# Converting 64-bit weights in seven VectorE instructions instead of nine, inside a Fourier and MoE kernel

## The chip, the cores and the metric

The kernel runs on one core of one Trainium2 chip. The metric is device time in microseconds for one execution, as the median of several runs. The runs of the kernel before took 2005.75, 2008.94 and 2009.99 us, so its median is 2008.94 us. The profiled execution is one more run, of 2006.93 us.

## The reference

Three layers follow one another on 4 x 3072 tokens of width 256. The code below leaves out the set-up of the inputs.

```python
# 1: Fourier layer
X = np.fft.rfft(x, axis=1)
Yr = X.real @ w_r - X.imag @ w_i + b_r
Yi = X.real @ w_i + X.imag @ w_r + b_i
Y = soft_threshold(Yr, 0.01) + 1j * soft_threshold(Yi, 0.01)
x = np.fft.irfft(Y, n=3072, axis=1)
# 2: MoE 1, w_in 256 x 2048, w_out 2048 x 256
h = x @ w_in
x = (h - np.tanh(h)) @ w_out
# 3: MoE 2, w_k 256 x 1024, w_v 1024 x 256, w_r 256 x 256
xk, xr = mix(x, x_prev, mu_k), mix(x, x_prev, mu_r)
k = np.maximum(xk @ w_k, 0.0)
out = sigmoid(xr @ w_r) * (k * k @ w_v)
```

The weights `w_in`, `w_out`, `w_k`, `w_v` and `w_r` of the two MoE layers arrive as 64-bit floats. The kernel reads each as a pair of 32-bit integers, a low and a high word side by side, and makes a 32-bit float of it.

## The kernel before, in words

**Stage 1** is the Fourier layer. The transform of length 3072 is split into factors 96 and 32. Each of the 4 batches has 12 *units* (`reg_unit`), so there are 48. A unit's work goes back and forth between the engines: `g` (TensorE, twiddles) to `xh`, `xl` (ScalarE and VectorE, the high and the low part of a value, lines 345 and 348), to `y` (TensorE, the weights `wh`, `wl`, two blocks of 12 matmuls), to `t` and `c` (VectorE, lines 529 to 534, bias and soft threshold), to `zh`, `zl` (ScalarE and VectorE), to `v` (TensorE, the inverse transform, two groups of three matmuls), to a copy and a store on ScalarE and SyncE's queue (`vdr`). A product of two 32-bit values is made from the high and low parts in three matmuls. When a batch is through, its `v` rows are loaded again as `vp`, multiplied by `e_sb` into `a` and stored as tokens (`ydr`, `reg_ap`). This work of batch b lies among the units of batch b+1, and that of the last batch among the first chunks of stage 2.

**Stage 2** (MoE 1) goes over 24 chunks of 512 tokens, with 8 pairs of weight slices in each. **Stage 3** is MoE 2. Both make products with fewer matmuls by using sums of blocks (`reg_forms`): for each slice of weights the kernel loads a 128 x 512 tile `ws` from DRAM (`stage`, line 690), adds and subtracts 128 x 256 blocks into `sq` (line 686), and splits these into high and low parts `ah`, `al`, `wh`, `wl`. The tokens get the same treatment: `yr` is loaded, `yt` holds the sums, and `yh`, `yl` the parts.

**The conversion** is `reg_conv(i)`, lines 597 to 632, once for each of 25 tiles of 128 x 512 weights. A DMA loads `raw`, 512 KB. Nine VectorE instructions make a 32-bit float of each pair. The result goes to DRAM as `wdr` (line 632, SyncE's queue), from where `stage` loads it as `ws`. The first 16 (`EARLY`: `w_in` and `w_out`) are converted during stage 1. Their load is issued on GpSimd's queue (line 613) into the one buffer of `raw` in the pool `px`; `cq` has two buffers there, `cs` and `cl` one each. The other 9 are converted in stage 2, with `raw` in the tile `sq` of the pool `pw` and the work tiles among the four buffers of `ws`. The pool `pw` takes the place of `px` (line 326), so the first load into `ws` can be issued only behind the last use of `px`, and that is the store of the last early conversion.

**Who sets the order.** Nothing is written down in the order in which it runs. Every instruction is registered with a priority and a cost in nanoseconds (`c_dve`, `c_act`, and for a DMA a fixed start of 650 ns, 290 bytes per ns on one common line and 950 ns to landing), and `_Plan.run` (lines 186 to 309) simulates the engines with these costs and emits each engine's instructions in the order of their simulated starts. On the chip each engine then runs its list in order. A different number of VectorE instructions, or a different last reader of a buffer, so gives other lists on all engines. Early conversions have priorities from 1000 on, which lets them into the gaps that the units leave in the simulation.

Of the kernel before, what the change touches and what calls it, by code (L numbers as in the profile page):

```python
# [8 lines left out]
F32 = mybir.dt.float32  # L9
F32R = mybir.dt.float32r  # L10
I32 = mybir.dt.int32
ACTF = mybir.ActivationFunctionType
ALU = mybir.AluOpType
# [135 lines left out]
class _Plan:  # L149
# [6 lines left out]
    def op(self, eng, dur, emit, prio, writes=(), reads=(), after=(), lat=SEM, seq=True, nbytes=0):  # L156
        o = _Op()
        o.nbytes = nbytes
        o.eng, o.dur, o.emit, o.prio, o.lat = eng, dur, emit, prio, lat
        o.idx = len(self.ops)  # L160
        o.start = o.end = None
        deps = set(after)
        o.creates, o.frees = [], []
        for t in reads:
            deps.update(t.writers)
            t.readers.append(o)
        for t in writes:
            if not t.writers:
                o.creates.append(t)
                if t.tag is not None:  # L170
                    self.rings.setdefault((t.pool, t.tag), []).append(t)
            elif seq:
                deps.add(t.writers[-1])
            else:
                deps.add(t.writers[0])
            t.writers.append(o)
            deps.update(r for r in t.readers if r is not o)
        for t in list(reads) + list(writes):
            if t.pool is not None:
                t.pool.ops.append(o)  # L180
        deps.discard(o)
        o.deps = deps
        self.ops.append(o)
        return o
# [127 lines left out]
def fourier_moe_kernel(tc, x, w_r, w_i, b_r, b_i, w_in, w_out, mu_k, mu_r, w_k, w_v, w_rr, c_f, c_e, c_t, c_b, out, nb=B, ydump=None):  # L312
# [3 lines left out]
    op = plan.op  # L316
# [18 lines left out]
    def tile_(pool_, shape, dtype, tag, bufs=1, ordered=True):  # L335
        return _Tile(pool_, shape, dtype, tag, bufs, ordered)
# [260 lines left out]
    def reg_conv(i):  # L597
        src, split = raws[i]
        if i < EARLY:
            w, q, s, l = (tile_(px, [128, n], I32, tag, k) for n, tag, k in ((1024, "raw", 1), (512, "cq", 2), (512, "cs", 1), (512, "cl", 1)))  # L600
            raw, q, s, l = (w, lambda: w().rearrange("p (c t) -> p c t", t=2)), (q, q), (s, s), (l, l)
            pr = 1000 + i
        else:
            w = tile_(pw, [128, 4, 256], F32, "sq", 1)
            raw = (w, lambda: w().bitcast(I32).rearrange("p a (c t) -> p (a c) t", t=2))
            q, s, l = ((t, lambda t=t: t().bitcast(I32)) for t in (tile_(pw, [128, 512], F32, "ws", 4) for _ in range(3)))
            pr = P2 + 8 * K["l0"] + 8 * K["l1"] * (i - EARLY)

        def load():
            o = raw[1]()  # L610
            if split:
                o = o.rearrange("p (f c) t -> p f c t", f=split)
            (pool if i < EARLY else sp).dma_start(out=o, in_=src)

        def ts(o, i_, s1, s2, o0, o1):
            if o1 is None:
                dve.tensor_scalar(out=o, in0=i_, scalar1=s1, scalar2=None, op0=o0)
            else:
                dve.tensor_scalar(out=o, in0=i_, scalar1=s1, scalar2=s2, op0=o0, op1=o1)

        dma("pool" if i < EARLY else "sp", load, pr, [raw[0]], [], 524288, after=[qt[divmod(RAW0 + i * RAW1 // 4, NU)].writers[0] if i < EARLY else yload[int(K["l0"] + K["l1"] * (i - EARLY))]])
        c1, c2 = c_dve(512, False), c_dve(512)
        op("dve", c1, lambda: ts(q[1](), raw[1]()[:, :, 1], 0x7FFFFFFF, None, ALU.bitwise_and, None), pr, [q[0]], [raw[0]])
        op("dve", c1, lambda: ts(s[1](), raw[1]()[:, :, 1], -(2 ** 31), None, ALU.bitwise_and, None), pr, [s[0]], [raw[0]])
        op("dve", c1, lambda: ts(l[1](), raw[1]()[:, :, 0], 9, None, ALU.logical_shift_right, None), pr, [l[0]], [raw[0]])
        op("dve", c1, lambda: ts(q[1]().bitcast(F32), q[1]().bitcast(F32), 2.0 ** -15, BIG, ALU.max, ALU.min), pr, [q[0]])
        op("dve", c1, lambda: ts(q[1](), q[1](), 3, 0x7FFFFFFF, ALU.logical_shift_left, ALU.bitwise_and), pr, [q[0]])
        op("dve", c2, lambda: dve.scalar_tensor_tensor(out=q[1](), in0=q[1](), scalar=0x40000000, in1=s[1](), op0=ALU.bitwise_xor, op1=ALU.bitwise_or), pr, [q[0]], [s[0]])
        op("dve", c1, lambda: ts(s[1](), q[1](), -(2 ** 23), None, ALU.bitwise_and, None), pr, [s[0]], [q[0]])
        op("dve", c2, lambda: dve.scalar_tensor_tensor(out=s[1]().bitcast(F32), in0=l[1](), scalar=2.0 ** -43, in1=s[1]().bitcast(F32), op0=ALU.mult, op1=ALU.mult), pr, [s[0]], [l[0]])  # L630
        op("dve", c2, lambda: dve.tensor_tensor(out=q[1]().bitcast(F32), in0=q[1]().bitcast(F32), in1=s[1]().bitcast(F32), op=ALU.add), pr, [q[0]], [s[0]])
        dma("sp", lambda: sp.dma_start(out=wdr_t[i], in_=q[1]().bitcast(F32)), pr, [wdr[i]], [q[0]], 262144)

# [418 lines left out]
```

## Time and profile before

| | before |
|---|---|
| median of 3 runs | 2008.94 us |
| lowest and highest run | 2005.75, 2009.99 us |
| profiled execution: its time, its span | 2006.93 us, 2005.1 us |
| TensorE busy | 1961.8 us, 98% of the span |
| VectorE busy | 1599.4 us, 80% |
| ScalarE busy | 1476.9 us, 74% |
| GpSimd busy | 22.9 us, 1% |
| mean granted TensorE clock | 0.993 |

The span runs from the first to the last instruction in the trace; the time of that execution is 1.83 us longer. "Busy" counts the time in which an engine has an instruction under way. Durations of consecutive VectorE instructions overlap by a few tens of nanoseconds, so the distance between two starts is a little shorter than a duration where nothing holds the second. In the trace, the time that an engine sat idle before an instruction stands in brackets with what ended the wait.

### The profile page before, as it was taken

Reading aid. Unit: us, or ns where it says so; the run is one execution under the profiler, and the core shown is the slowest. Engines: PE = TensorE matmul, PEld = TensorE weight load, DVE = VectorE, ACT = ScalarE, POOL = GpSimd, SP = SyncE. Lnnn points to the kernel's source line nnn. Section 1 sums busy time; section 2 is a strip of 40 time slices with the busy share of each in tenths; the row PEclk is TensorE's granted clock in tenths of the full one; section 3 lists DMA queues with packets and bytes.
Section 4 is the critical chain, followed back from the end, with each engine's and each line's share of the span. In section 5 each row is a group of like instructions: output and inputs, shape, how many; then the busy total and the mean of one; then the engine's idle time right before and its main releaser. Section 6 shows DMA issues by size and latency. Waiting matters only on the chain.

```text
span 2005.1 us, 36620 instructions
## 1 busy us (share of the span) xinstructions
PE 1961.8 (98%) x13760; PEld 1822.3 (91%) x13760; DVE 1599.4 (80%) x3107; ACT 1476.9 (74%) x3166; POOL 22.9 (1%) x42
## 2 busy tenths in 40 slices
PE   5999999999999999999999999999999999999998
PEld 3899989888888888888888888888999999999998
DVE  1688897788887878887878897779988888888885
ACT  3657566777777777777777787778877777777774
POOL 2000000000000000000000000000000000000000
PEclk8999999999999999999999999999999999999999
DMA  9699786511010101010101120001211111111101
GB/s 311 197 288 295 242 264 217 179 48 55 29 47 24 37 22 48 32 38 22 38 22 48 38 69 22 22 11 35 60 44 50 48 47 47 47 47 47 47 22 33
DMA packets 96194, 162.37 MB, mean 81 GB/s; under 512 B 11510, under 2 KB 56675, under 8 KB 96016
## 3 DMA queue, kind: packets, MB, share of 16 engines
q1 hardware_dynamic: 91008, 142.95, 22.8%
q0 software_dynamic: 4112, 13.93, 2.4%
q10 hardware_dynamic: 896, 3.15, 0.4%
q8 instruction: 108, 1.77, 0.4%
q14 instruction: 70, 0.57, 0.1%
HBM read 90.52 MB, written 69.47 MB: 80 GB/s over the span
## 4 chain that ended last, share of the span: by engine, by line
PE 89%; DVE 5%; DMA 3%; ACT 2%; issue 1%; SPq 0%; ACTq 0%; DVEq 0%
PE v L319 39%; PE y L319 20%; PE g L319 17%; PE a L319 14%; DVE hs L840 1%; DVE hs L799 1%; DVE yl L348 1%; DMA x<-in_x_dram 1%; DMA adr<-at 1%; DVE gl L348 1%; DMA ydr<-yt 0%; DMA out_dram<-ob 0%; DVE zl L348 0%; DMA vp<-vdr 0%; DMA yr<-ydr 0%
## 5 line engine op out<-in xcount | busy, mean ns | idle before, releaser
L345 ACT ACTIVATE gh<-hs 128x512 fp32r<-128x512 f32 x504 | 317.2, 629 | 139.2 <-PE v L319 131.4
L348 DVE TENSOR_TENSOR gl<-hs,gh 128x512 fp32r<-128x512 f32 x504 | 345.1, 685 | 79.5 <-ACT gh L345 79.1
L796 ACT ACTIVATE p<-g 128x256 f32<-128x256 f32 x864 | 318.7, 383 | 92.8 <-PE g L319 75.0
L840 DVE TENSOR_TENSOR hs<-hs,th 128x512 f32<-128x512 f32 x384 | 264.4, 689 | 122.1 <-ACT th L839 115.1
L319 PE MATMUL v<-gh,wl 128*128 128x512 f32 x768 | 303.6, 395 | 0.0
L319 PE MATMUL v<-gh,wh 128*128 128x512 f32 x768 | 303.3, 395 | 0.0
L319 PE MATMUL v<-gl,wh 128*128 128x512 f32 x768 | 300.0, 391 | 0.0
L839 ACT ACTIVATE th<-hs 128x512 f32<-128x512 f32 x384 | 241.5, 630 | 76.2 <-DVE hs L799 71.6
L799 DVE TENSOR_TENSOR hs<-y,p 128x256 f32<-128x256 f32 x588 | 241.4, 420 | 37.1 <-PE y L319 25.8
L319 PE MATMUL v<-ah,gh 128*128 128x256 f32 x768 | 217.5, 283 | 0.5 <-DVE ob L1004 0.5
L319 PE MATMUL v<-al,gh 128*128 128x256 f32 x768 | 217.3, 283 | 0.0
L319 PE MATMUL v<-ah,gl 128*128 128x256 f32 x768 | 217.3, 283 | 0.0
L319 PE MATMUL g<-yh,ah 128*128 128x256 f32 x648 | 183.2, 283 | 0.1
L319 PE MATMUL g<-yh,al 128*128 128x256 f32 x648 | 182.8, 282 | 0.0
L319 PE MATMUL g<-yl,ah 128*128 128x256 f32 x648 | 182.5, 282 | 0.0
L319 PEld LDWEIGHTS v<-gl,wh 128*128 128x128 f32 x768 | 144.4, 188 | 33.4
L319 PEld LDWEIGHTS v<-gh,wh 128*128 128x128 f32 x768 | 145.2, 189 | 18.1
L319 PEld LDWEIGHTS v<-gh,wl 128*128 128x128 f32 x768 | 145.2, 189 | 16.0
L319 PE MATMUL y<-yh,ah 128*128 128x256 f32 x496 | 149.8, 302 | 2.6 <-ACT hs L824 1.0
L319 PEld LDWEIGHTS v<-ah,gh 128*128 128x128 f32 x768 | 147.4, 192 | 0.8 <-DVE ob L1004 0.7
L319 PEld LDWEIGHTS v<-al,gh 128*128 128x128 f32 x768 | 147.4, 192 | 0.0
L319 PEld LDWEIGHTS v<-ah,gl 128*128 128x128 f32 x768 | 147.4, 192 | 0.0
(179 smaller groups left out, 4875.9 us busy)
## 6 DMA issues: line engine op xcount, KB each, us to landing
x<-in_x_dram SPq DMA_DIRECT2D x32, 384.0 KB, 5.2
q<-adr SPq DMA_DIRECT2D x48, 256.0 KB, 5.8
vdr<-v SPq DMA_DIRECT2D x48, 256.0 KB, 3.6
vp<-vdr SPq DMA_DIRECT2D x32, 384.0 KB, 6.3
ydr<-yt SPq DMA_DIRECT2D x64, 192.0 KB, 4.5
yr<-ydr SPq DMA_DIRECT2D x24, 512.0 KB, 4.0
xdr<-x SPq DMA_DIRECT2D x24, 512.0 KB, 3.1
xs<-xdr SPq DMA_DIRECT2D x20, 608.0 KB, 4.3
```

The costliest lines, as they stand in the source:

```text
L319: pe.matmul(out=o, lhsT=l, rhs=r, start=st, stop=en, **kw)
L345: op("act", c_act(n, psum), lambda: act.activation(out=o[1](), in_=i[1](), func=ACTF.Copy), prio, [o[0]], [i[0]])
L348: op("dve", c_dve(n), lambda: dve.tensor_tensor(out=o[1](), in0=i[1](), in1=h[1]().bitcast(F32), op=ALU.subtract), prio, [o[0]], [i[0], h[0]])
L796: op("act", c_act(HK, True), lambda: act.activation(out=o(), in_=p()[:, 0:HK], func=ACTF.Copy), prio, [o], [p])
L799: op("dve", c_dve(HK), lambda: dve.tensor_tensor(out=t()[:, half * HK:half * HK + HK], in0=p()[:, 0:HK], in1=s(), op=ALU.add), prio, [t], ...
L839: op("act", c_act(CK, False), lambda th=th, hs=hs: act.activation(out=th(), in_=hs(), func=ACTF.Tanh), z0, [th], [hs])
L840: op("dve", c_dve(CK), lambda th=th, hs=hs: dve.tensor_tensor(out=hs(), in0=hs(), in1=th(), op=ALU.subtract), z0, [hs], [th])
```

## The change

In `reg_conv`, three instructions read `raw` before: the magnitude of the high word (`cq`), its sign bit (`cs`), and the low word shifted right by 9 (`cl`). Now only the first of them is left. The mask behind the shift is one bit narrower, and the fourth instruction takes the two top bits straight from the high word in `raw` and joins them to `cq`. The sixth takes the low word straight from `raw`, read as an unsigned integer, and scales it by 2^-52 instead of scaling the shifted word by 2^-43. The tile `cl` is gone, and the late conversions take two buffers of `ws` instead of three. Line numbers behind line 617 are one lower in the changed kernel.

```diff
--- before.py
+++ after.py
@@ -597,13 +597,13 @@
     def reg_conv(i):
         src, split = raws[i]
         if i < EARLY:
-            w, q, s, l = (tile_(px, [128, n], I32, tag, k) for n, tag, k in ((1024, "raw", 1), (512, "cq", 2), (512, "cs", 1), (512, "cl", 1)))
-            raw, q, s, l = (w, lambda: w().rearrange("p (c t) -> p c t", t=2)), (q, q), (s, s), (l, l)
+            w, q, s = (tile_(px, [128, n], I32, tag, k) for n, tag, k in ((1024, "raw", 1), (512, "cq", 2), (512, "cs", 1)))
+            raw, q, s = (w, lambda: w().rearrange("p (c t) -> p c t", t=2)), (q, q), (s, s)
             pr = 1000 + i
         else:
             w = tile_(pw, [128, 4, 256], F32, "sq", 1)
             raw = (w, lambda: w().bitcast(I32).rearrange("p a (c t) -> p (a c) t", t=2))
-            q, s, l = ((t, lambda t=t: t().bitcast(I32)) for t in (tile_(pw, [128, 512], F32, "ws", 4) for _ in range(3)))
+            q, s = ((t, lambda t=t: t().bitcast(I32)) for t in (tile_(pw, [128, 512], F32, "ws", 4) for _ in range(2)))
             pr = P2 + 8 * K["l0"] + 8 * K["l1"] * (i - EARLY)
 
         def load():
@@ -620,14 +620,13 @@
 
         dma("pool" if i < EARLY else "sp", load, pr, [raw[0]], [], 524288, after=[qt[divmod(RAW0 + i * RAW1 // 4, NU)].writers[0] if i < EARLY else yload[int(K["l0"] + K["l1"] * (i - EARLY))]])
         c1, c2 = c_dve(512, False), c_dve(512)
-        op("dve", c1, lambda: ts(q[1](), raw[1]()[:, :, 1], 0x7FFFFFFF, None, ALU.bitwise_and, None), pr, [q[0]], [raw[0]])
-        op("dve", c1, lambda: ts(s[1](), raw[1]()[:, :, 1], -(2 ** 31), None, ALU.bitwise_and, None), pr, [s[0]], [raw[0]])
-        op("dve", c1, lambda: ts(l[1](), raw[1]()[:, :, 0], 9, None, ALU.logical_shift_right, None), pr, [l[0]], [raw[0]])
+        high = lambda: raw[1]()[:, :, 1]
+        op("dve", c1, lambda: ts(q[1](), high(), 0x7FFFFFFF, None, ALU.bitwise_and, None), pr, [q[0]], [raw[0]])
         op("dve", c1, lambda: ts(q[1]().bitcast(F32), q[1]().bitcast(F32), 2.0 ** -15, BIG, ALU.max, ALU.min), pr, [q[0]])
-        op("dve", c1, lambda: ts(q[1](), q[1](), 3, 0x7FFFFFFF, ALU.logical_shift_left, ALU.bitwise_and), pr, [q[0]])
-        op("dve", c2, lambda: dve.scalar_tensor_tensor(out=q[1](), in0=q[1](), scalar=0x40000000, in1=s[1](), op0=ALU.bitwise_xor, op1=ALU.bitwise_or), pr, [q[0]], [s[0]])
+        op("dve", c1, lambda: ts(q[1](), q[1](), 3, 0x3FFFFFFF, ALU.logical_shift_left, ALU.bitwise_and), pr, [q[0]])
+        op("dve", c2, lambda: dve.scalar_tensor_tensor(out=q[1](), in0=high(), scalar=-(2 ** 30), in1=q[1](), op0=ALU.bitwise_and, op1=ALU.bitwise_or), pr, [q[0]], [raw[0]])
         op("dve", c1, lambda: ts(s[1](), q[1](), -(2 ** 23), None, ALU.bitwise_and, None), pr, [s[0]], [q[0]])
-        op("dve", c2, lambda: dve.scalar_tensor_tensor(out=s[1]().bitcast(F32), in0=l[1](), scalar=2.0 ** -43, in1=s[1]().bitcast(F32), op0=ALU.mult, op1=ALU.mult), pr, [s[0]], [l[0]])
+        op("dve", c2, lambda: dve.scalar_tensor_tensor(out=s[1]().bitcast(F32), in0=raw[1]()[:, :, 0].bitcast(mybir.dt.uint32), scalar=2.0 ** -52, in1=s[1]().bitcast(F32), op0=ALU.mult, op1=ALU.mult), pr, [s[0]], [raw[0]])
         op("dve", c2, lambda: dve.tensor_tensor(out=q[1]().bitcast(F32), in0=q[1]().bitcast(F32), in1=s[1]().bitcast(F32), op=ALU.add), pr, [q[0]], [s[0]])
         dma("sp", lambda: sp.dma_start(out=wdr_t[i], in_=q[1]().bitcast(F32)), pr, [wdr[i]], [q[0]], 262144)
 
```

The lists of the engines are the same up to the first conversion, at about 116 us of the span, and TensorE's is the same again over the second half of the program; between them they differ. Three places follow.

The first is VectorE among the first units of the fourth batch, at the last two of the 16 early conversions (`t` and `c` up to `zl` are the units' own chain). Before, from the 16th's `cq<-raw` to its last row:

```order
L617 TENSOR_SCALAR cq<-raw 128x512
L619 TENSOR_SCALAR cq<-cq 128x512
L348 TENSOR_TENSOR zl<-t,zh 128x512
L619 TENSOR_SCALAR cq<-cq 128x512
L628 SCALAR_TENSOR_TENSOR cq<-cq,cs 128x512
L529 TENSOR_TENSOR t<-y,bias 128x512
L348 TENSOR_TENSOR xl<-g,xh 128x4x128
L533 TENSOR_SCALAR c<-t 128x512
L617 TENSOR_SCALAR cs<-cq 128x512
L534 TENSOR_TENSOR t<-t,c 128x512
L630 SCALAR_TENSOR_TENSOR cs<-cl,cs 128x512
L631 TENSOR_TENSOR cq<-cq,cs 128x512
```

and in the changed kernel, where the first two rows end the 15th conversion and the third begins the 16th:

```order
L629 SCALAR_TENSOR_TENSOR cs<-raw,cs 128x512
L630 TENSOR_TENSOR cq<-cq,cs 128x512
L617 TENSOR_SCALAR cq<-raw 128x512
L619 TENSOR_SCALAR cq<-cq 128x512 x2
L529 TENSOR_TENSOR t<-y,bias 128x512
L348 TENSOR_TENSOR xl<-g,xh 128x4x128
L533 TENSOR_SCALAR c<-t 128x512
L627 SCALAR_TENSOR_TENSOR cq<-raw,cq 128x512
L534 TENSOR_TENSOR t<-t,c 128x512
L617 TENSOR_SCALAR cs<-cq 128x512
L629 SCALAR_TENSOR_TENSOR cs<-raw,cs 128x512
L348 TENSOR_TENSOR zl<-t,zh 128x512
```

Before, the 16th conversion ends within the third unit of the batch. In the changed kernel it begins behind that unit, right behind the 15th's last two rows, the first of which is the last reader of the 15th's `raw`, and it ends within the fifth unit.

The second is VectorE at the last unit of the third batch, in the changed kernel:

```order
L629 SCALAR_TENSOR_TENSOR cs<-raw,cs 128x512
L534 TENSOR_TENSOR t<-t,c 128x512
L630 TENSOR_TENSOR cq<-cq,cs 128x512
L348 TENSOR_TENSOR zl<-t,zh 128x512
L529 TENSOR_TENSOR t<-y,bias 128x512
L533 TENSOR_SCALAR c<-t 128x512
L534 TENSOR_TENSOR t<-t,c 128x512
L617 TENSOR_SCALAR cq<-raw 128x512
L348 TENSOR_TENSOR zl<-t,zh 128x512
```

The first row is the last reader of the 13th conversion's `raw`, and the 14th's `cq<-raw` stands seven rows behind it and ahead of the `zl` on which the batch's last `v` waits. Before, the row in this place belonged to the 15th conversion and stood behind that `zl`.

The third is TensorE at the change from stage 1 to stage 2. Before (`y<-wh,xh` and the two rows under it are the second block of the last unit's `y`; `g<-yh,ah` and what follows are products of stage 2):

```order
L319 MATMUL y<-wh,xh 128x256 x4
L319 MATMUL y<-wl,xh 128x256 x4
L319 MATMUL y<-wh,xl 128x256 x4
L319 MATMUL g<-yh,ah_3741 128x256
L319 MATMUL g<-yh,al_3748 128x256
L319 MATMUL g<-yl,ah_3741 128x256
L319 MATMUL g<-yh,ah_3741 128x256
L319 MATMUL g<-yh,al_3748 128x256
L319 MATMUL g<-yl,ah_3741 128x256
L319 MATMUL y<-yh,ah_3741 128x256
```

and in the changed kernel, where the last block of `y` ends four rows above the first of these rows:

```order
L319 MATMUL v<-zl,b_628 128x256
L319 MATMUL v<-zh,b_628 128x256 x2
L319 MATMUL v<-zl,b_628 128x256
L319 MATMUL v<-zh,b_628 128x256 x2
L319 MATMUL v<-zl,b_628 128x256
L319 MATMUL v<-zh,b_628 128x256 x2
L319 MATMUL v<-zl,b_628 128x256
L319 MATMUL v<-zh,b_628 128x256 x2
L319 MATMUL v<-zl,b_628 128x256
L319 MATMUL g<-yh,ah_3807 128x256
L319 MATMUL g<-yh,al_3809 128x256
```

Before, nine matmuls of stage 2 stand between the last `y` and the `v` of the last two units. In the changed kernel the `v` of the last three units stand together, and stage 2 begins behind all of them.

## Rows read from the trace of the kernel before

**Rows 1.** Busy time of each engine, its share of the span and its instructions, on the page.

```profile
PE 1961.8 (98%) x13760; PEld 1822.3 (91%) x13760; DVE 1599.4 (80%) x3107; ACT 1476.9 (74%) x3166; POOL 22.9 (1%) x42
```

**Rows 2.** Stretches of the span: length, busy us (instructions) by engine, clock, DMA.

```profile
0.00:50.00 50.00, 28.92 (x112) 18.08 (x113) 4.95 (x9) 16.50 (x35) 12.76 (x27) 0.83 0.97 311
50.00:300.00 250.00, 240.94 (x1860) 231.10 (x1859) 203.22 (x385) 157.34 (x334) 10.17 (x15) 0.99 0.81 257
350.00:400.00 50.00, 47.56 (x347) 44.11 (x346) 38.56 (x79) 40.00 (x92) 0.00 (x0) 1.00 0.58 180
400.00:1800.00 1400.00, 1396.97 (x9398) 1283.09 (x9397) 1158.42 (x2251) 1088.17 (x2323) 0.00 (x0) 1.00 0.13 39
1800.00:2005.00 205.00, 197.39 (x1625) 196.01 (x1623) 156.38 (x313) 144.30 (x319) 0.00 (x0) 0.99 0.15 40
```

**Rows 3.** Groups of the early conversions' VectorE instructions, 100 to 320 us: busy us, mean ns.

```profile
L630 DVE SCALAR_TENSOR_TENSOR cs<-cl,cs 128x512 f32<-128x512 int32 x16 | 11.0, 686 | 0.2
...
L617 DVE TENSOR_SCALAR cq<-raw 128x512 int32<-128x512 int32 x16 | 6.7, 420 | 6.4 <-DMA raw<-in_moe_w_in_dram 3.3 <-DMA raw<-in_moe_w_out_dram 3.1
...
L617 DVE TENSOR_SCALAR cl<-raw 128x512 int32<-128x512 int32 x16 | 6.7, 418 | 0.0
```

**Rows 4.** Tile raw on GpSimd's queue: who held its loads, and their time to landing.

```profile
  DVE cl L617: 245.4, 15
...
DMA to landing us min/median/max: 4.4/6.2/13.8
```

**Rows 5.** Timeline of VectorE from 130 us: start, us, instruction, idle before and releaser.

```profile
134.69 0.43 DVE L617 TENSOR_SCALAR cq<-raw 128x512 int32<-128x512 int32 x1 [2.62 <-DMA raw<-in_moe_w_in_dram]
```

**Rows 6.** Timeline of TensorE at the two changes of batch, from 193 and from 277 us.

```profile
193.86 0.39 PE L319 MATMUL v<-zl,b 128*128 128x256 f32 x1 [0.42 <-DVE zl L348]
...
194.43 1.95 PE L319 MATMUL g<-t,q 128*128 128x128 f32 x16
...
277.85 0.50 PE L319 MATMUL v<-zh,b 128*128 128x256 f32 x2 [2.46 <-ACT zh L345]
279.06 0.58 PE L319 MATMUL v<-zl,b 128*128 128x256 f32 x1 [0.71 <-DVE zl L348]
...
280.08 2.85 PE L319 MATMUL g<-t,q 128*128 128x128 f32 x16
283.90 1.16 PE L319 MATMUL g<-t,q 128*128 128x128 f32 x8 [0.96 <-ACT xh L504]
```

**Rows 7.** Stretches of the later change of batch, columns as in rows 2.

```profile
275.00:280.00 5.00, 1.84 (x10) 1.43 (x9) 4.96 (x12) 1.23 (x2) 0.00 (x0) 0.86 0.92 272
280.00:285.00 5.00, 4.04 (x27) 3.85 (x26) 3.78 (x9) 3.04 (x8) 0.72 (x1) 0.80 1.10 386
```

**Rows 8.** Timelines of SyncE's queue and of VectorE behind the last early conversion.

```profile
301.51 0.82 SPq L632 DMA_DIRECT2D wdr<-cq  x1
...
304.98 0.47 SPq L690 DMA_DIRECT2D ws<-wdr  x1
...
309.64 0.69 DVE L529 TENSOR_TENSOR t<-y,bias 128x512 f32<-128x512 f32 x1 [7.42 <-PE y L319]
```

**Rows 9.** Timeline of TensorE at the change from stage 1 to stage 2.

```profile
348.44 0.64 PE L319 MATMUL y<-wh,xl 128*128 128x256 f32 x4
348.91 0.28 PE L319 MATMUL g<-yh,ah 128*128 128x256 f32 x1
...
350.59 0.50 PE L319 MATMUL v<-zh,b 128*128 128x256 f32 x2 [0.45 <-ACT zh L345]
351.31 0.39 PE L319 MATMUL v<-zl,b 128*128 128x256 f32 x1 [0.23 <-DVE zl L348]
...
357.77 0.38 PE L319 MATMUL y<-yh,ah 128*128 128x256 f32 x1 [1.04 <-ACT hs L824]
```

**Rows 10.** Timeline of VectorE in the same place, one instruction of each size.

```profile
336.23 1.22 DVE L348 TENSOR_TENSOR yl<-yt,yh 128x1024 fp32r<-128x1024 f32 x1
...
355.00 0.42 DVE L799 TENSOR_TENSOR hs<-y,p 128x256 f32<-128x256 f32 x1
355.34 1.22 DVE L348 TENSOR_TENSOR al<-sq,ah 128x1024 fp32r<-128x1024 f32 x1
356.48 0.69 DVE L348 TENSOR_TENSOR wl<-ws,wh 128x512 fp32r<-128x512 f32 x1
357.09 0.68 DVE L840 TENSOR_TENSOR hs<-hs,th 128x512 f32<-128x512 f32 x1
```

## Prediction

> **What bounds the kernel now.** Read the busy times first: TensorE is busy for 98% of the span, VectorE for 80% [rows 1]. So work taken off VectorE is worth only what TensorE waits for it. Then read the same by stretches [rows 2], length less TensorE's busy time: 21.1 us idle in the first 50 us, 9.1 from 50 to 300, 2.4 from 350 to 400, 3.0 in the 1400 us of stages 2 and 3 up to 1800, and 7.6 at the end. The first conversion stands at 116 us and the lists are equal until then, so the 21.1 us stay, and so does the drain at the end, where no conversion stands. What is left to win is some 11 us at the changes of batch and of stage (9.1 + 2.4, of which a part lies before 116 us). What can be lost has no such limit: any place where TensorE's list comes to something that VectorE has not yet done.
>
> **The change part by part: the instructions.** An instruction with one source takes 418 to 420 ns, one with two 686 ns [rows 3]. Two of the first kind go from each of 25 conversions: 25 x 2 x 0.42 = 21 us less on VectorE at most, 13.4 of it in stage 1. All of it lies beside TensorE's work, so by itself it counts as nothing; the waits below say where it shows.
>
> The two instructions that now read `raw` themselves take every second word of it. The trace of before has no two-source instruction that does so. Below, the cost is that of the row nearest to it in form, 686 ns [rows 3]; above, I add the whole duration of one more pass, 0.42 us, to each of the two. I take 686 ns, because the one-source `cq<-raw` and `cl<-raw`, which read every second word, take 420 and 418 ns, no more than the ones that read packed tiles. The Trainium skill speaks against the change here (Vector Engine (DVE) Microarchitecture Reference, section Measured stream behaviour on trn2): a port keeps its rate only for runs of two adjacent words, and one source that hops every element costs 1.73 instead of 1.05 ns per column. By that estimate each of the two would take 0.35 us longer, and the saving of the conversion would be gone; the rows above show no such price for one source, and no run shown here has it for two.
>
> **The buffer.** There is one `raw` buffer, and GpSimd's queue waited for the last reader `cl` before each of 15 loads, 245 us in all [rows 4]. Before, `cl` stands among the first instructions of a conversion; now the last reader is the sixth of seven. A load takes 4.4 to 13.8 us, in the median 6.2 [rows 4], while the planner assumes 0.65 + 1.8 + 0.95 = 3.4 us. So each next conversion begins later, and where the plan puts its first instruction right behind that last reader, VectorE's list stands still for most of a load. Before it did so for 2.62 us at the third conversion [rows 5]. I go through TensorE's list at the four places where this can reach it.
>
> *First batch.* The third conversion's first instruction stands two rows behind the second's last reader. That reader ends at about 130.6 us, against 128.3 for the load's issue before, so VectorE goes on at 137 instead of 134.7 [rows 5], and the `xl` behind it is some 2 us late for a `y`: +2 us (0 to 4, with a load of 4.4 or 8).
>
> *Change from the second batch to the third.* The last unit's chain and two more conversion steps stand before its `zl`; walked through with 0.34 us from start to start for a one-source instruction and 0.61 for two sources [rows 10], TensorE waits about 1.6 us where it waited 0.42 [rows 6] and a little more: +1 us (-0.5 to +2).
>
> *Change from the third to the fourth.* Before, TensorE waited 2.46, 0.71 and 0.96 us [rows 6], and its 16 `g` took 2.85 us where the same 16 took 1.95 a batch earlier [rows 6], at a granted clock of 0.86 and 0.80 [rows 7], so part of these 10 us ran at the lower of the clock's two levels, 1.2 GHz, behind the gap. Three conversion instructions fewer stand in the last unit's chain, but the 14th conversion's first one stands ahead of its `zl`, with a load issued some 3.5 us earlier. With 6.2 us for the load the waits come to about 5, but TensorE puts fewer `g` behind them and loses less clock: passing takes 1.5 us less than before (-3 at 4.4 us for the load, +2 at 8).
>
> *Change from stage 1 to stage 2, the largest term.* Before, the last early result was issued to DRAM at 301.51 and the first weights came back under an issue at 304.98, 3.5 us later; VectorE then idled 7.42 us [rows 8]. That slack is what hides the early conversions. In the changed kernel the 16th conversion waits a whole load right behind the 15th and ends two units later. The units stand 6.3 us apart there, so its result leaves at about 316, the first weights are asked for at about 320 and used at 324. The slack is gone, and VectorE has the sums and parts of stage 2 to make in 15 us less time, together with the last units. The planner knows this and puts three units' `v` in front of the first product of stage 2, where before nine products stood between them and TensorE waited 0.45 + 0.23 us, and 1.04 later [rows 9]. Call X the end of the last `y`. VectorE still has 20 instructions to go, from the last unit's `t` to the `yl` of 1024 columns that the second product needs and that was done at 337.5, 11 us before X, in the kernel before [rows 9, 10]. They are 7 with two sources and 512 columns, one with one source, 9 of 256 columns and 3 of 1024, at 0.61, 0.34, 0.34 and 1.14 us from start to start [rows 10]: 4.3 + 0.3 + 3.1 + 3.4 = 11.1 us, and some 0.6 for the `zl` that wait for ScalarE. TensorE has 18 matmuls of `v` and 6 of the first product until then, 24 x 0.12 = 2.9 us. It waits 11.7 - 2.9 = 8.8 us, plus the small waits for `hs` that are there before too, plus up to 1 us at the lower clock as behind the earlier gap [rows 6, 7]. Against the 0.7 us of before I take +8.5 us. The bounds are +3, if VectorE gets ahead of this list while TensorE still does `y`, and +14, if the first weights come so late that X finds VectorE some 5 us behind.
>
> *Stage 2.* The nine late conversions save 9 x 0.84 = 7.6 us of VectorE, where TensorE idles 3 us in 1400 [rows 2]: 0, or -1 at best.
>
> The sum: 2 + 1 - 1.5 + 8.5 = +10 us on the profiled execution's 2006.93 us, which is 2017 us. The median of the runs is 2008.94, 2 us above that execution, so 2017 is 8 us above the median, 0.4%.
>
> **The rivals.** (a) *Faster, the slack holds.* What decides is when the first weights of stage 2 come back. If the loads of `raw` take 4.4 us, the 15th and 16th conversions end some 4 us earlier, VectorE meets X with its list short, and the transition costs no more than before; then the third change of batch gives its 3 us and the early places cost nothing: 2007 - 3 = 2004 us. For it: VectorE has 13 us less to do up to there. Against it: the list, not the load, puts the `yl` 20 rows behind, and TensorE can't pass the `v`.
>
> (b) *No change that can be measured.* The transition costs its lower bound of 3, the rest cancels: 2007 + 3 = 2010 us. For it: TensorE is full at 98% and has the same work.
>
> (c) *Two-source reads at every second word are slow.* Then 16 x 2 x 0.42 = 13 us come back to VectorE in stage 1, and each conversion's last reader is up to 0.8 us later; the walk gives 1 us more at each of two changes of batch and 2 at the transition: 2021 us. The rows of one source speak against it [rows 3]. The Trainium skill's rule above is this case.
>
> **How the numbers follow.** A measurement of this kernel can tell about 0.2%, 4 us, from no change. The forecast gets 0.56, (c) 0.10, (b) 0.21 and (a) 0.13. So slower 0.66, same 0.21, faster 0.13. The range takes in the forecast with its bounds, (c) and most of (b): the terms' upper ends together would be +22, which is not likely all at once; I go to 2026, and down to 2005.
>
> **What would show it.** Right: in the changed kernel's profile VectorE waits several us for `raw` at the third and the 16th conversion; the first `ws<-wdr` is issued at about 320 us; TensorE stands idle for some 8 us in two or three pieces behind the last `y` of stage 1, released by `zl` and `yl`; from 400 us on nothing differs. The new instructions take 0.69 us. Wrong: that transition without a wait over 2 us, or the first `ws<-wdr` before 312; new instructions of 0.9 us or more; or a difference that arises behind 400 us.

## The result, and the profile after

The changed kernel is slower: 2024.48 us in the median of 6 runs (2021.3 to 2028.53), against 2009.3 us for the kernel before in as many runs beside it. The ratio is 1.0077, with a 95% interval of 1.0063 to 1.0092. The forecast was 2017 us, so the direction and the range held and the size did not: 15 us came instead of 8. The profiled execution took 2021.3 us, with a span of 2019.5. It is the fastest of the six, so the accounts below, made on profiled executions, explain 14.4 of the 15.2 us between the medians.

**The busy times**, from the page of the changed kernel:

```profile
span 2019.5 us, 36574 instructions
PE 1969.7 (98%) x13760; PEld 1829.7 (91%) x13760; DVE 1587.3 (79%) x3057; ACT 1478.2 (73%) x3166; POOL 22.3 (1%) x42
```

Against [rows 1] VectorE has 50 instructions and 12.1 us less. TensorE has the same 13760 matmuls and is busy 7.9 us longer. So a part of the loss hides inside "busy"; below it is traced to the clock.

**The stretches** of the changed kernel, columns as in [rows 2]:

```profile
0.00:50.00 50.00, 28.77 (x97) 17.86 (x98) 3.82 (x7) 15.78 (x34) 12.78 (x27) 0.80 0.97 311
50.00:300.00 250.00, 239.23 (x1821) 228.91 (x1821) 185.26 (x336) 154.50 (x326) 8.77 (x14) 0.98 0.78 247
350.00:400.00 50.00, 42.14 (x300) 39.49 (x299) 38.07 (x78) 34.99 (x76) 0.00 (x0) 0.86 0.66 206
400.00:1800.00 1400.00, 1397.53 (x9372) 1282.71 (x9371) 1156.01 (x2236) 1086.30 (x2322) 0.00 (x0) 1.00 0.13 38
```

TensorE idles 7.9 us between 350 and 400 us where it idled 2.4, and the clock there fell from 1.00 to 0.86. From 400 to 1800 us there is no loss: 2.5 us idle against 3.0. So the loss lies in stage 1 and at its end.

**The instructions.** The groups of VectorE in the early conversions of the changed kernel:

```profile
L629 DVE SCALAR_TENSOR_TENSOR cs<-raw,cs 128x512 f32<-128x512 uint32 x16 | 11.0, 687 | 0.2
L627 DVE SCALAR_TENSOR_TENSOR cq<-raw,cq 128x512 int32<-128x512 int32 x16 | 11.0, 686 | 0.2
...
L617 DVE TENSOR_SCALAR cq<-raw 128x512 int32<-128x512 int32 x16 | 6.8, 422 | 20.1 <-DMA raw<-in_moe_w_out_dram 12.7 <-DMA raw<-in_moe_w_in_dram 7.3
```

The two-source instructions that read every second word take 686 and 687 ns, as the packed one did [rows 3]. The Trainium skill's rule of 1.73 instead of 1.05 ns per column for a source that hops 4 KiB at every element (Vector Engine (DVE) Microarchitecture Reference, section Measured stream behaviour on trn2) does not show for this step of two words: by an estimate from that page, 512 columns would have taken some 350 ns more. What changed is the last row's idle time: VectorE waits 20.1 us for `raw`, against 6.4 [rows 3].

**The buffer**, tile `raw` on GpSimd's queue in the changed kernel:

```profile
  DVE cs L629: 274.3, 15
...
DMA to landing us min/median/max: 4.4/6.4/13.8
```

As announced, the last reader is now `cs`, and the loads themselves are as slow as before [rows 4]. VectorE stands still at three places for half a load or more each, and at three more for under 1 us each. From its timeline:

```profile
140.48 0.43 DVE L617 TENSOR_SCALAR cq<-raw 128x512 int32<-128x512 int32 x1 [7.29 <-DMA raw<-in_moe_w_in_dram]
...
223.54 0.43 DVE L617 TENSOR_SCALAR cq<-raw 128x512 int32<-128x512 int32 x1 [4.71 <-DMA raw<-in_moe_w_out_dram]
...
314.57 0.43 DVE L617 TENSOR_SCALAR cq<-raw 128x512 int32<-128x512 int32 x1 [5.75 <-DMA raw<-in_moe_w_out_dram]
```

These are the 3rd, the 9th and the 16th conversion. What TensorE makes of it stands in its own timeline. First the two places inside batches and the third change of batch:

```profile
143.04 1.16 PE L319 MATMUL g<-t,q 128*128 128x128 f32 x8 [1.30 <-ACT xh L504]
...
227.67 1.13 PE L319 MATMUL a<-e_sb,vp 96*128 96x96 f32 x8 [2.44 <-ACT yt L572]
...
285.69 0.50 PE L319 MATMUL v<-zh,b 128*128 128x256 f32 x2 [0.30 <-ACT zh L345]
286.96 0.39 PE L319 MATMUL v<-zl,b 128*128 128x256 f32 x1 [0.77 <-DVE zl L348]
```

The wait at 227.67 names ScalarE, but ScalarE was itself held. Its timeline:

```profile
226.85 0.38 ACT L504 ACTIVATE xh<-g 128x256 fp32r<-128x256 f32 x1 [2.88 <-DVE xl L348]
227.13 0.48 ACT L572 ACTIVATE yt<-a 128x384 f32<-128x384 f32 x1
```

The copy `yt` that TensorE needs stands behind an `xh` that waits for VectorE's `xl`, and that `xl` stands behind the `cq<-raw` at 223.54. A wait for a load on VectorE so reaches TensorE over ScalarE's list.

Second, the change from stage 1 to stage 2 on TensorE:

```profile
353.87 0.64 PE L319 MATMUL y<-wh,xl 128*128 128x256 f32 x4
...
356.49 0.50 PE L319 MATMUL v<-zh,b 128*128 128x256 f32 x2 [1.26 <-ACT zh L345]
357.83 0.38 PE L319 MATMUL v<-zl,b 128*128 128x256 f32 x1 [0.84 <-DVE zl L348]
...
359.82 0.80 PE L319 MATMUL v<-zh,b 128*128 128x256 f32 x2 [1.26 <-ACT zh L345]
...
366.85 0.58 PE L319 MATMUL g<-yh,ah 128*128 128x256 f32 x1 [3.95 <-ACT yh L345]
...
368.11 0.58 PE L319 MATMUL g<-yl,ah 128*128 128x256 f32 x1 [0.46 <-DVE yl L348]
```

The five waits come to 7.77 us, against 0.45 + 0.23 + 1.04 and one smaller before [rows 9]. What the gaps do to the clock stands in the stretches of the two worst places, columns as above:

```profile
225.00:230.00 5.00, 2.56 (x20) 2.40 (x19) 4.96 (x9) 2.41 (x6) 0.73 (x1) 0.93 0.84 273
230.00:235.00 5.00, 5.00 (x35) 5.00 (x34) 0.02 (x1) 0.27 (x1) 0.00 (x0) 0.73 0.80 249
...
355.00:360.00 5.00, 1.65 (x9) 1.03 (x9) 5.00 (x11) 3.62 (x8) 0.00 (x0) 0.90 0.29 100
360.00:365.00 5.00, 2.81 (x9) 1.96 (x9) 4.66 (x10) 2.66 (x5) 0.00 (x0) 0.50 0.48 154
365.00:370.00 5.00, 2.69 (x11) 2.40 (x12) 3.88 (x9) 2.84 (x6) 0.00 (x0) 0.50 0.93 282
370.00:375.00 5.00, 5.00 (x35) 5.00 (x35) 3.30 (x9) 3.50 (x7) 0.00 (x0) 0.74 1.03 257
```

Busy time times the missing share of the clock gives an estimate of what the lower level (1.2 GHz) costs: 5.00 x 0.27 + 2.56 x 0.07 = 1.5 us at the first place, and 1.65 x 0.1 + (2.81 + 2.69) x 0.5 + 5.00 x 0.26 = 4.2 us at the second. With 1.7 us at the start (last section) and 0.3 more than before at the third change of batch (below) that is 7.7 of the 7.9 us by which TensorE is busy longer.

**The queue.** SyncE's list in the changed kernel, last early result and first weights of stage 2:

```profile
322.53 0.32 SPq L631 DMA_DIRECT2D wdr<-cq  x1
...
323.83 0.46 SPq L689 DMA_DIRECT2D ws<-wdr  x1
```

They come 21.0 and 18.9 us later than before [rows 8]. TensorE's last `y` of stage 1 ended at 354.4 (its last four matmuls start at 353.87, above), 30.5 us behind that first `ws`; in the kernel before, 44 us lay between the two [rows 8, 9].

### The profile page after: what moved, and what is told of

Read it like the earlier page. It is cut to its first block, busy times and chain, and to the rows that moved or that the text cites. A ratio compares the mean times of both kernels' runs of the same rounds, so it can differ in the third digit from the quotient of the medians.

```text
span 2019.5 us, 36574 instructions
## 1 busy us (share of the span) xinstructions
PE 1969.7 (98%) x13760; PEld 1829.7 (91%) x13760; DVE 1587.3 (79%) x3057; ACT 1478.2 (73%) x3166; POOL 22.3 (1%) x42
## 4 chain that ended last, share of the span: by engine, by line
PE 83%; DVE 5%; DMA 1%; ACT 1%; issue 0%; DVEq 0%; ACTq 0%; SPq 0%
PE v L319 39%; PE y L319 17%; PE g L319 16%; PE a L319 12%; DMA raw<-in_moe_w_out_dram 1%; DVE hs L839 1%; DVE yl L348 1%; DVE hs L798 1%; DVE gl L348 0%; DMA raw<-in_moe_w_in_dram 0%; ACT yh L345 0%; DVE zl L348 0%; ACT hs L823 0%; DVE t L534 0%; DVE cq L619 0%
```

## The experiments

The forecast's theory was: the late release of `raw` costs, through waits for loads and through late weights of stage 2. The rivals: the instructions themselves cost; or neither, and the lists that the planner makes from the changed costs and readers are simply worse. Each ratio is against runs of the kernel before on the same chip.

| run | edit | median us | ratio, 95% interval |
|---|---|---|---|
| changed kernel | | 2024.48 | 1.0077 [1.0063, 1.0092] |
| e1_two_raw | two `raw` buffers | 2014.65 | 1.0029 [1.0019, 1.0039] |
| e2_late_list_two_raw | two buffers, lists unchanged | 2015.2 | 1.0040 [1.0025, 1.0055] |
| e3_nine_list | seven instructions in the lists of nine | 2008.02 | 0.9995 [0.9987, 1.0004] |
| e4_nine_late | kernel before, planned with late release | 2027.84 | 1.0102 [1.0084, 1.0119] |
| e5_seven_early | seven, planned with early release | 2019.43 | 1.0058 [1.0041, 1.0074] |
| e6_nine_cheap | kernel before, cost figure x 0.81 | 2017.1 | 1.0047 [1.0032, 1.0062] |
| e7_raw0_8 | loads of `raw` from 6 units earlier | 2014.46 | 1.0034 [1.0021, 1.0047] |
| e8_two_raw0_8 | e1 and e7 together | 2017.45 | 1.0052 [1.0037, 1.0067] |
| e9_moved | e3, four instructions held back | 2009.72 | 1.0005 [0.9997, 1.0014] |
| e10_nine_097 | kernel before, cost figure x 0.97 | 2014.69 | 1.0033 [1.002, 1.0046] |
| e11_nine_103 | kernel before, cost figure x 1.03 | 2004.45 | 0.9977 [0.9968, 0.9986] |
| e12_seven_103 | changed kernel, cost figure x 1.03 | 2022.99 | 1.0078 [1.0061, 1.0095] |

### The instructions alone: e3

In the planner the two removed instructions stay, with their cost and as readers of `raw`, but emit nothing; so every other instruction stands where it stood before. The planner counts one buffer, the chip has two.

```diff
+        op("dve", c1, lambda: None, pr, [s[0]], [raw[0]])
+        op("dve", c1, lambda: None, pr, [l[0]], [raw[0]])
...
-bufs=self.bufs
+bufs=2 if self.tag == "raw" else self.bufs
```

> The seven instructions in the list of the kernel before: the planner still reckons with nine and with raw free after the third, the two that are gone issue nothing, and raw has two buffers on the chip, so that the loads can start where they did. TensorE's, ScalarE's and SyncE's lists are those of before word for word. Release theory: nothing is lost; VectorE has 21 us less to do, of which TensorE gets at most the removable waits: 2002 to 2009 us, the gain at the change from the third batch to the fourth, where two or three instructions fewer stand in front of zl (TensorE's wait there 2.5 to 3.5 instead of 4.1 us). Instruction rival: above 2015 us.

It gives 0.9995, no difference. VectorE was busy 1586.2 us, 13 us less than before. The gain expected at the third change of batch did not come: TensorE's waits there are those of before [rows 6], as its timeline in e3 shows:

```profile
280.17 0.50 PE L319 MATMUL v<-zh,b 128*128 128x256 f32 x2 [2.54 <-ACT zh L345]
281.38 0.39 PE L319 MATMUL v<-zl,b 128*128 128x256 f32 x1 [0.71 <-DVE zl L348]
```

So the seven instructions, in the old lists and with two buffers, neither gain nor lose anything. The Trainium skill's advice to minimize the count of chained VectorE operations (VectorE: DVE Perf Modes, section Rules for kernel authors) gained nothing here: two instructions less in each of 25 conversions left the time as it was. The whole loss of the change comes from lists and release.

### The real wait for the buffer: e2 and e1

e2 keeps the changed kernel's lists word for word and gives the chip a second `raw` buffer that the planner doesn't know of; e1 lets the planner know. Parts of the changed lines:

```diff
# e2
-bufs=self.bufs
+bufs=2 if self.tag == "raw" else self.bufs
# e1
-(1024, "raw", 1)
+(1024, "raw", 2)
```

> Every engine's list as in the changed kernel, word for word, but raw has two buffers on the chip, so that a load no longer waits for the sixth instruction. It tells the real wait for a load from the list. Release theory: the two losses in the middle of stage 1, where TensorE waits behind VectorE's wait for raw (at 143 and 228 us, 1.3 and 2.4 us and some lower clock), go, 3 to 6 us; the list still puts three units' v in front of stage 2 and the yl of 1024 columns behind them, so most of the 8 us of waits at the change to stage 2 and the lower clock behind them stay: 2016 to 2021 us. Wait rival (the real waits for loads are the whole loss): 2006 to 2011 us. List rival (the list is the whole loss): 2022 to 2026 us.

> The seven-instruction conversion with two raw buffers instead of one, planned with two. Release theory (the loss comes from raw being free only after the sixth instruction): with a second buffer the next load no longer waits for that reader, the 16th conversion ends within the third unit of the fourth batch as before, the first load of stage 2's weights is issued near 305 us, TensorE waits under 3 us at the change to stage 2, VectorE waits under 4 us for raw in all; 2004 to 2010 us, no slower than the kernel before. Instruction rival (the new two-source reads, or the seven instructions themselves, cost the time): still above 2018 us. List rival (any change of the planned list loses by chance): anywhere from 2005 to 2025 us, with waits at other places.

e2 came out at 1.0040, a little under its expectation. VectorE has no wait for `raw` left, and the loss inside the batches is gone. The transition is not. Stretches and TensorE's timeline in e2:

```profile
225.00:230.00 5.00, 5.00 (x46) 5.00 (x45) 1.44 (x3) 1.24 (x3) 0.72 (x1) 1.00 1.02 294
...
355.00:360.00 5.00, 1.11 (x4) 0.55 (x3) 3.57 (x6) 3.12 (x5) 0.00 (x0) 0.50 0.64 205
```

```profile
349.69 0.50 PE L319 MATMUL v<-zh,b 128*128 128x256 f32 x2 [1.26 <-ACT zh L345]
...
360.05 0.58 PE L319 MATMUL g<-yh,ah 128*128 128x256 f32 x1 [3.95 <-ACT yh L345]
361.31 0.58 PE L319 MATMUL g<-yl,ah 128*128 128x256 f32 x1 [0.46 <-DVE yl L348]
```

The five waits (1.26, 0.84, 1.25, 3.95 and 0.46 us) are the changed kernel's to 0.01 us. So the waits on the chip for the one buffer cost 0.0077 - 0.0040 = 0.0037 of the time, 7.4 us (with the two intervals joined, 7.4 +/- 4.2), and the transition does not hang on them: its waits come with the lists.

e1 missed its expectation of at most 2010 us; what came is the list rival's case. With two buffers planned, no wait for `raw` is left (VectorE waits 2.8 us for stores of `cq` instead) and the first `ws` is issued at 307.16, but other places broke. From TensorE's timeline in e1:

```profile
199.20 1.01 PE L319 MATMUL g<-t,q 128*128 128x128 f32 x3 [3.32 <-DMA q<-adr]
...
286.02 3.78 PE L319 MATMUL g<-t,q 128*128 128x128 f32 x16 [0.84 <-DMA q<-adr]
290.76 3.78 PE L319 MATMUL g<-t,q 128*128 128x128 f32 x16 [0.96 <-ACT xh L504]
```

Now the unit's operand `q` is late, and 32 `g` run at 3.78 us for 16, where the same 16 took 1.95 [rows 6].

### The list alone: e4, e5, e6

e4 is the kernel before, in which the planner is told that the eighth of a conversion's nine instructions still reads `raw`, so that it plans the late release with nine instructions. e5 plans seven instructions with early release (e3 with the two empty steps at no cost). e6 is the kernel before with the planner's cost of a conversion's instructions lowered to about the sum of seven, and nothing else. Parts of the changed lines:

```diff
# e4
-pr, [s[0]], [l[0]])
+pr, [s[0]], [l[0], raw[0]])
# e5, against e3
-op("dve", c1, lambda: None,
+op("dve", 0, lambda: None,
# e6
-c1, c2 = c_dve(512, False), c_dve(512)
+c1, c2 = c_dve(512, False) * 0.81, c_dve(512) * 0.81
```

> The nine instructions of before, unchanged on the chip, but the planner is told that raw is read until the eighth. The release on the chip is early as before, the list is that of a late release. Release theory: the list alone moves the conversions back (the 16th ends within the sixth unit of the fourth batch), the first load of stage 2's weights comes near 325 us or later, and TensorE waits 8 us or more at the change to stage 2: 2017 to 2028 us, with VectorE's waits for raw shorter than in the changed kernel. Instruction rival and wait rival: 2005 to 2011 us, as before.

> The seven instructions with two raw buffers on the chip, planned as seven instructions but with raw free after the first of them, so that the planner sees the shorter work and not the later release. The list is a new one from unit 13 on. Release theory: the shorter work by itself doesn't move the early conversions back, the 16th ends in the third unit of the fourth batch as before, TensorE waits under 3 us at the change to stage 2: 2003 to 2012 us. Rival (any new list loses by chance as much as the changed kernel's): 2015 us or more.

> A control: the nine instructions and the early release of before, only the planner's cost of a conversion instruction is lowered by 19%, so that the list is shuffled by as much shorter work and by nothing else. Release theory: within 0.3% of the kernel before, 2004 to 2015 us, with no wait over 3 us at the change to stage 2. Rival (lists by chance): as far off as the changed kernel, 2016 us or more, is as likely as not.

e4 is the slowest of all, 1.0102, with no wait of VectorE for `raw`: the time, and over 8 us of waits at the change to stage 2, are what the release theory had forecast. The first `ws` is issued only at 349.43, 7 us ahead of the end of the last `y`. The wait itself is for `vp`, at a place that no conversion feeds: the list puts the last batch's own `a<-e_sb` ahead of the first product of stage 2. SyncE's list and TensorE's timeline in e4:

```profile
349.43 1.87 SPq L690 DMA_DIRECT2D ws<-wdr  x4
```

```profile
217.18 8.16 PE L319 MATMUL a<-e_sb,vp 96*128 96x96 f32 x40 [2.25 <-DMA vp<-vdr]
...
356.06 0.64 PE L319 MATMUL y<-wh,xl 128*128 128x256 f32 x4
...
371.74 8.85 PE L319 MATMUL a<-e_sb,vp 96*128 96x96 f32 x40 [9.06 <-DMA vp<-vdr]
```

e5 and e6 missed: 1.0058 and 1.0047, where the theory of the late release, which neither has, gave no more than 2012 and 2015 us; in both the rival of lists by chance came out. In e5 TensorE loses at `a<-e_sb` behind `vp` (2.11 us and a lower clock after it) and at the third change of batch. In e6 it loses above all at that change, in its timeline:

```profile
281.37 0.58 PE L319 MATMUL v<-zl,b 128*128 128x256 f32 x1 [2.52 <-DVE zl L348]
...
284.30 0.80 PE L319 MATMUL v<-zh,b 128*128 128x256 f32 x2 [1.71 <-ACT zh L345]
```

e6 is the control: a cost figure changed, no instruction and no reader, and the kernel is slower by more than half of what the change cost. A list of this planner is good or bad by chance to about that extent.

### Loads earlier: e7 and e8

```diff
-RAW0, RAW1 = 14, 6
+RAW0, RAW1 = 8, 6
```

> The changed kernel with its one buffer, but the first load of raw is allowed six units earlier (8 instead of 14), so that the 16th conversion ends in the tenth unit of the third batch. Release theory: the slack behind the conversions is back, the first load of stage 2's weights is issued before 300 us, the waits and the lower clock at the change to stage 2 go (9 us less), VectorE still waits for raw where the list puts the next conversion right behind the last reader: 2008 to 2017 us. Wait rival: no better than the changed kernel by more than 4 us, 2020 us or more.

> Two raw buffers and the earlier start together, seven instructions. Release theory: neither waits for raw nor waits at the change to stage 2; what is left are the changes of batch: 2002 to 2010 us, and the best chance of a version under the kernel before. Rival (lists by chance): anywhere up to 2020 us, with the loss at a change of batch behind a load of q.

e7 halves the loss, to 1.0034, within its forecast. The first `ws` is issued at 291.65, and the transition's waits are 0.45, 0.23, 0.16 and 1.04 us, those of before [rows 9]. VectorE still waits 10.5 + 7.4 us for `raw`. The largest loss is now at the change from the second to the third batch, in TensorE's timeline of e7:

```profile
199.81 0.79 PE L319 MATMUL v<-zh,b 128*128 128x256 f32 x2 [2.24 <-ACT zh L345]
204.28 3.76 PE L319 MATMUL g<-t,q 128*128 128x128 f32 x16 [2.53 <-DMA q<-adr]
```

e8, without any wait for `raw`, missed its forecast of 2002 to 2010 us and is no better (1.0052). Its loss is the rival's, at a change of batch behind a load of `q`: 3.17 us for `zh` at 198.77, 4.06 for `q` at 204.77, and both following runs of 16 `g` at 3.57 us or more.

### One wait moved by hand, and the cost figure: e9 to e12

e9 takes e3 and emits the last four instructions of the 14th conversion only behind the third batch's last `zl`, to win the 2.5 us of that change.

```diff
+        if i == 13:
+            for o in plan.ops[-4:]:
+                o.hold = last_zl
```

> The seven instructions in the list of before with two raw buffers (as in the run with nine planned instructions), and the last four instructions of the 14th conversion moved by hand from between the t and c of the third batch's last unit to behind its zl. Every other list is untouched. Release theory and list theory agree here: the zl of that unit comes about 1.6 us earlier on VectorE, TensorE's waits at that change of batch fall from 4.6 to about 2.5 us and less of it is run at the lower clock: 2003 to 2008 us, 1 to 4 us under the run without the move. If the waits there are set by ScalarE's zh or by the q that is loaded, nothing changes: 2006 to 2010 us.

Nothing was won (1.0005), the case that the forecast had set apart for waits set by `zh` or `q`. The wait for `zh` fell from 2.54 to 1.85 us, and the `q` behind it is late instead; TensorE in e9, whose line numbers are 10 higher:

```profile
281.62 3.79 PE L329 MATMUL g<-t,q 128*128 128x128 f32 x16 [1.79 <-DMA q<-adr]
```

e10, e11 and e12 shift the same cost figure as e6 by 3%: down and up in the kernel before, up in the changed one.

> A second control: the nine instructions and buffers of before, with the planner's cost of a conversion instruction 3% lower. List theory (the list of before is an unusually good one, and nearly any other loses): 2011 to 2018 us although neither the work nor the release differs. Release theory alone: 2005 to 2011 us.

> A third control: as the second, with the cost 3% higher. List theory: 2011 to 2018 us. Release theory alone: 2005 to 2011 us.

> The changed kernel, one buffer and late release on the chip and in the plan, with the planner's cost of a conversion instruction 3% higher. Its lists are those of the changed kernel up to unit 16; then the 16th conversion ends in the third unit of the fourth batch, as in the kernel before, and products of stage 2 stand ahead of the last units' v again. Two-part theory (the changed kernel loses some 9 us to real waits for raw in stage 1 and some 6 us to the place where its list puts the early conversions' end): the second part goes and the first stays, 2013 to 2020 us, VectorE waits more than 12 us for raw, TensorE under 3 us at the change to stage 2. If the late release alone is the loss: 2020 us or more, as in the changed kernel. If the list alone is: 2003 to 2012 us.

e10 is slower by 0.33%, as the list theory said. e11 is faster by 0.23%, just under both of its forecasts: the best version found, and faster than both kernels. In e11 the third change of batch keeps its clock, in its stretch from 250 to 300 us, where the clock was 0.97 in the kernel before and in the changed one, and 0.90 in e1 and e10:

```profile
250.00:300.00 50.00, 47.43 (x355) 44.70 (x354) 47.28 (x94) 32.34 (x71) 3.13 (x4) 1.00 0.78 252
```

e12 missed its forecast of 2013 to 2020 us, and its 16th conversion ends in the fourth unit of the batch, not in the third. It is as slow as the changed kernel, 1.0078, though its transition costs little (3.2 us of waits in the 25 us behind the last `y`, against 7.8 in the changed kernel and 1.9 in the kernel before) and its loss lies elsewhere, at 193 (`zl`, 1.41 us), 230 (`yt`, 1.47) and 290 us (`zh`, 2.81). What it shares with the changed kernel is the wait of VectorE for the one buffer, here 11.8 + 11.3 us in nine pieces. Its first `ws` and its last `y` of stage 1, on SyncE's queue and on TensorE:

```profile
323.94 0.92 SPq L689 DMA_DIRECT2D ws<-wdr  x2
```

```profile
363.18 0.64 PE L319 MATMUL y<-wh,xl 128*128 128x256 f32 x4
```

The `ws` is as late as in the changed kernel, but here the last `y` ends 39.7 us behind it, not 30.5.

### What follows

The three kernels that release one buffer late on the chip (the changed one, e7, e12) stand at 1.0034 to 1.0078. The ten that do not stand between 0.9977 (e11) and 1.0102 (e4), and the kernel before (1) lies among the better of them. The two groups overlap, so only kernels with the same list tell the real wait from the list: the changed kernel and e2. By these, 7.4 +/- 4.2 of the change's 15 us are the real wait for `raw`, and the rest a worse list. e3, in the old lists, shows that nothing is left for the instructions.

Where that list loses, at the transition, one number goes with the waits in all the profiles: the time from the first issue of `ws` to the end of the last `y` of stage 1. It is 30.5 us in the changed kernel and in e2, with 7.8 us of TensorE's waits in the 25 us behind that `y`; 7 us in e4, with 12.2; and 39.7 to 81 us in the kernel before and in the other ten runs, with 1.9 to 3.2. e7, which only lets the loads begin earlier, has 64 us and the waits of before. So the transition's loss goes with late weights, and e4, whose edit tells the planner of the late release and nothing else, shows that the planner then makes them late. Every edit that moved the weights moved the lists too, so the weights alone were not tried. The total is not explained by this: e5, e6, e8 and e10 lose 0.33 to 0.58% at other places, and how much of the changed kernel's list is such chance stays open. The join of the top bits and the reading of the low word were not tried apart; e3 shows that both together cost nothing.

## Why the prediction was right and wrong

| term | forecast, us | in the traces, us |
|---|---|---|
| batch 1, behind the 3rd conversion | +2 | +1.3 |
| second to third batch | +1 | about +0.5 |
| 9th conversion, inside a batch | not seen | +4.0 |
| third to fourth batch | -1.5 | -2.0 |
| stage 1 to stage 2 | +8.5 | about +10 |
| start, ahead of any conversion | 0 | +1.9 |
| stage 2 and the rest | 0 | about -1.3 |
| sum | +10 | +14.4 |

The column on the right is TensorE's waits, plus the clock's loss as worked out above, less the same of the kernel before. The last row but one is what is left of the measured sum.

- **The instructions at 686 ns, worth nothing by themselves: right.** Measured in the groups above, and alone in e3. The rival of slow reads falls. Of the "21 us less on VectorE at most" 12.1 were measured, beside TensorE as said.
- **The buffer: right.** The 3rd and the 16th conversion wait, as said, 7.29 and 5.75 us.
- **"I go through TensorE's list at the four places where this can reach it": the first step that failed.** There was a fifth. At the 9th conversion VectorE waits 4.71 us, and over `xl`, `xh` and `yt` TensorE stood 2.44 us and lost 1.5 us of clock behind that, 4.0 in all. I had looked for `cq<-raw` close behind the release only at the changes and at the first conversions, and had not followed every one of the 16 to what stands behind it on ScalarE too.
- **Third to fourth batch: right.** Waits of 0.16, 0.22, 0.31, 0.30 and 0.77 us and 1.4 us of clock stand against 4.13 and 1.1 us before [rows 6, 7].
- **Stage 1 to stage 2: right in place and in the list, wrong in two sizes that partly cancel.** VectorE had the 20 instructions of the walk to do, but from the end of the last `y` to the end of the `yl` passed 13.7 us instead of 11.7: an `al` stood in front, and VectorE waited 2.0 us for ScalarE, not 0.6, of which the last is this row of its timeline:

```profile
366.83 1.23 DVE L348 TENSOR_TENSOR yl<-yt,yh 128x1024 fp32r<-128x1024 f32 x1 [1.12 <-ACT yh L345]
```

TensorE's waits were still 7.77 us for a forecast of 8.8, because its 24 matmuls, in broken pieces and mostly at the lower clock, took some 6 us instead of 2.9. The step "plus up to 1 us at the lower clock as behind the earlier gap" is the mis-sized term: it measured 4.2 us. About 2 of them lie among those waits, where a faster TensorE would mostly have waited longer (argued from the lists, not tried), and about 2 behind them. The earlier gap was 2.46 us with 0.71 and 0.96 in the 6 us behind it [rows 6]; here five gaps lay within 12 us, and the clock was 0.50 from 360 to 370.
- **Why the transition got this list: it fits, but the weights alone were not tried.** I put it down to weights asked for at 320 us, which leave no slack (323.83 measured). The slack, from that issue to the end of the last `y`, goes with the waits in all the profiles, as said above, and e7 and e4 moved both together.
- **The start: not in the prediction, and no effect of the change**; see the last section. Without it the profiled difference is 12.5 us, for a forecast of 10: the terms that were too low (the 9th conversion, the clock) outweigh those that were too high.

## What to carry to other kernels

When instructions are fused, look first at which of them was the last reader of a single buffer: here two instructions less cost 0.37 +/- 0.21% in waits, because the load behind the buffer began later, and follow each such wait to every engine that stands in line behind it. Where a planner sets the order, run the same instructions in the old lists, and the old instructions with a cost moved by 3%, before a difference under 1% is put down to the change: such a shift gave -0.23% and +0.33% here. A gap on a full TensorE is to be priced with its clock: at the places above, 0.26 to 0.8 us came on top of each us of wait.

## What was unexpected of the hardware

The lists are the same up to the first conversion, yet the profiled executions are 1.9 us apart there: the first `t` of stage 1 starts on VectorE at 47.34 us in the kernel before and at 49.20 in the changed one. The three matmuls that open the `y` in front of it, in TensorE's timeline of the kernel before:

```profile
44.29 0.62 PE L319 MATMUL y<-wh,xh 128*128 128x256 f32 x3 [0.84 <-ACT xh L504]
```

and of the changed kernel:

```profile
44.43 1.01 PE L319 MATMUL y<-wh,xh 128*128 128x256 f32 x3 [0.75 <-ACT xh L504]
```

They start 0.14 us apart, and the same work takes 0.62 and 1.01 us: the clock rose later. Read in stretches of 1 us, the granted clock was 0.50 until about 43 us in the kernel before and until about 48.4 in the changed one. In other runs whose lists are equal so far the same `t` started at 47.25 us (e10), 47.41 (e4), 49.51 (e12), 49.77 (e6) and 50.54 (e11, the fastest kernel of all, where the first `g` also began 1 us later than in the kernel before). The Trainium skill says that the moment at which the clock rises is not tied to the kernel's start, and so varies (TensorE: Matmul & The Clock Gate, section Part 1: The HAM clock gate). The traces agree that it varies, and show what it can be worth here: 1.7 us between two executions that began the same work 0.14 us apart. In a comparison of two profiles, that offset is to be read at a point ahead of the change and taken off first.
